# A fused attention and two-expert-layer kernel: another written-out order for its first block, three value sums made on TensorE, two second products in split form, routing's vector work pinned in place

## The chip, the cores and the metric

The program runs on one core of a Trainium2 chip. The metric is the device time of one execution in microseconds (us). Before the change the median of 3 runs is 1375.94 us (1375.69 to 1376.54). Engines are named as the profile names them: PE (TensorE matmuls), PEld (its weight loads), DVE (VectorE), ACT (ScalarE), POOL (GpSimd) and SP (SyncE, which issues all the DMAs here).

## The reference, cut to what matters

Attention over pooled keys and values, a dense layer pair with softplus, then a layer of 8 experts of which each token takes the best one:

```python
# q, k, v: 8 batches x 8 heads x 576 x 64; k_p and v_p: means over 8 neighbours, so 72 keys
scores = scale * q @ k_p.T;  attn = softmax(scores);  a = attn @ v_p
x = a as 4608 tokens x 512
h = x @ w_in                                   # 512 x 2048
g = maximum(h, 0) + log1p(exp(-abs(h)))        # softplus
x = g @ w_out                                  # 2048 x 512
logits = (x / |x|) @ (emb / |emb|).T / tau     # 8 experts
idx = argmax(logits);  gate = max softmax(logits)
out = gate * (maximum(x @ w1[idx], 0) @ w2[idx])   # 512 x 1024 x 512
```

## The kernel before, in words

The 4608 tokens go in 9 blocks of 512. A product of two float32 matrices is made of parts rounded to the fp32r type: a value is its high part plus a rest, and `three` (lines 655 to 658) makes three fp32r matmuls, low by high, high by low and high by high. A matmul on whole float32 operands shows in the trace as two PE records.

For each block `mm1` makes h chunk by chunk (16 chunks of 128 of the 2048 columns; 12 matmuls of 512 columns a chunk), `softplus` (lines 669 to 694) runs over ACT (abs, exp, ln) and DVE, and `mm2` adds g times w_out into four PSUM tiles `acc`. Two PSUM buffers hold h, so the third chunk in a row waits for the softplus of the first. In block 0 every chunk is "full" (`FULL`, line 1169): softplus ends after one DVE addition (L686), and `mm2` multiplies the unrounded float32 g and w_out (L710, four matmuls a chunk). In later blocks g is split (DVE L689, ACT L691, DVE L693) and w_out too (`split_wo`: ACT L634, then DVE or POOL L638), and `mm2` takes `three`.

The first block also prepares everything: it loads q, k and v, sums k and v over 8 neighbours (`add`: on DVE as one reduction, L186, or on POOL as a tree of three additions, L200 to L202, chosen by the table `ALT`), makes masked sums and rounds them (`prep_v` and `build_v` make VH and VL; `prep_r` and `build_r` make RV from the 16 keys of each pair of heads that do not fit in 128 rows), transposes q and k on PE, makes scores and softmax (`score`), and multiplies by the values (`av`, into `pv`, whose result ACT and DVE split into the first input x, L436 and L438). It also turns the 64-bit weights of both dense layers into float32 (`conv_in`, `conv_out`: long chains on DVE, ACT and POOL, lines 587 to 628). All this is cut into small steps; the string `ORDER` lists them in the order in which the instructions are put on all engines, so each engine runs them in that order. A letter is a kind (K keys, B transposed keys, V and W values, R and U left-over values, Q, S scores, E, T, X attention output, I and O weights, M first product, G softplus, Z w_out's split, P second product, lower case a load, H a transpose of the identity that keeps PE working while it would wait). The last two second products of block 0 are not in the string; the main loop makes them among block 1's first products.

From block 1 on, PE and SP follow the code's order; a scheduler orders DVE, ACT and POOL. `route` (lines 758 to 799) turns a block's logits into gates and expert choice by some 15 tiny DVE instructions with one POOL instruction (L768, a square root by power) among them; after the last dense block it runs while the expert layer's first products (`mm3s`, PSUM tiles m, DVE lines 1042 to 1060) are under way.

The few lines that carry the argument:

```python
    def mm2(blk, fc):                     # block 0: float32 operands; else three fp32r products
        ...
            if full:
                nc.tensor.matmul(accs[blk][d], wof[fc][:, dd], f32(g)[:, 0, :], ...)
            else:
                three(accs[blk][d], w[:, 0, dd], w[:, 1, dd], g[:, 0, :], g[:, 1, :], ...)
```

Of the kernel before, what the change touches and what calls it, by code (L numbers as in the profile page):

```python
# [20 lines left out]
def tile_attention_moe_moe(  # L21
# [13 lines left out]
    nc = tc.nc  # L35
# [633 lines left out]
    def softplus(blk, fc):  # L669
# [9 lines left out]
        g_t[blk, fc] = g  # L679
        if alt(f"G{fc}.relu") and blk == 0:  # L680
# [78 lines left out]
    def route(blk):  # L759
# [408 lines left out]

    FULL = tuple(range(NFC))
# [12 lines left out]
    ORDER = """  # L1182
        k0.0 k0.1 l0 q1 K0 q0 H H H H H H H H H H H H H H H H H H H H H H H H H H H H H H H H Q1 K0 r0 k1.0 K0
        K0 K0 K0 K0 H H B0 Q1 q2 B0 Q0 B0 k1.1 B0 R0 S1 q3 S1 R0 S1 Q0 S0 K1 S0 S1 S1 v0.0 S1 Q2 K1 S1 Q2 S0
        K1 S0 H H H H H H S2 H H Q3 S2 l1 S1 U0 S0 S1 U0 Q3 S2 i6 H S3 S0 S2 U0 S1 K1 S1 S2 S3 S0 E1 S3 S2 S0
        K1 E1 q4 v0.1 K1 S2 K1 S0 H H H T1 V0 T1 S3 S0 S3 I6 T1 S2 S3 H H H B1 Q4 B1 I6 B1 S2 Q4 T1 V0 i0 B1
        I6 S3 S0 i2 V0 q5 V0 H H H H H H H H H S4 T1 q6 E0 E0 S2 S4 i3 I0 o6 T0 H H H H H H H H H H Q5 S3 S4
        T1 S3 T0 S4 q7 S4 I0 I0 i8 T0 S4 S2 W0 T0 Q6 o0 W0 U0 W0 T0 S4 r1 S3 W0 T0 i9 S4 I6 H H H H X1 i13 Q5
        S4 E2 X0 S3 Q6 I6 E3 X2 I2 I8 E2 X1 E3 X0 X2 I0 X1 X3 X0 X3 S4 X2 T2 T2 T2 X3 T3 T3 T2 Q7 v1.0 S6 T2
        T3 I0 T2 S4 i11 S6 T3 T3 T3 S6 I6 S5 X4 E4 I0 E4 Q7 I0 X4 S6 X5 S6 X6 i12 X5 X4 S6 I2 I9 o2 X5 X7 I2  # L1190
        X6 M0 X7 X6 T4 I6 X7 I8 I2 M0 R1 T4 T4 I11 O0 R1 T4 I2 S6 I12 M6 S6 T4 I2 T4 I13 S7 I13 O6 o13 S6 T4
        S5 I13 i10 S5 G6 G6 I13 I2 S5 U1 S5 O6 S6 M0 X10 G6 M0 S6 T4 I13 X10 G0 G0 X10 X9 X11 G6 T4 X11 S7 O6
        S7 S5 I13 G0 O0 - X11 E6 I8 X9 T4 S5 E6 v1.1 O13 V1 I11 O2 M2 O0 i7 G0 T6 o1 O2 I13 X9 O13 I3 O2 S7 O6
        M13 O13 O6 O0 S7 I11 I8 P6 O0 I10 I9 G2 V1 G13 P6 G2 I10 O2 I8 I7 I8 O2 I10 I9 o9 G2 o8 G13 I9 I12 I9
        G2 i5 I9 G13 P0 I9 S7 i4 S5 I11 P0 I10 O8 O9 P2 O8 P2 O9 O1 S5 O13 M9 X8 O8 I7 I4 I8 O13 I12 I4 G13 S7
        U1 I3 I10 o7 P13 M8 X8 O9 O8 O9 S5 I10 X8 O8 I5 T6 I10 G9 V1 O9 G9 S5 G9 o10 G9 P13 o11 G8 T6 I11 T6
        G8 U1 I11 E5 O7 S7 G8 I7 O11 I12 M10 O10 E5 P9 U1 G8 P9 O1 O7 G10 I11 T6 O10 O11 I7 O11 O10 I4 I5 G10
        I5 O10 G10 I7 I7 I12 T6 P8 V1 W1 I7 O10 M11 W1 G10 o4 S7 G11 T5 I4 S7 O1 T5 W1 G11 o5 I12 M7 G11 O1 I4
        O4 W1 G7 I12 P8 O7 O11 O7 I4 I4 i1 T5 G11 O4 S7 P10 O7 I3 M4 T5 G7 T5 G7 O11 T5 X14 o12 O5 O4 X14 O1
        O12 i14 O4 P11 O12 G4 G7 I14 X14 I14 O12 X13 I3 I5 I1 O4 E7 I1 X13 X15 I5 I14 I5 G4 O5 O5 G4 O5 G4 M12  # L1200
        P7 I3 X13 o3 P10 X12 O12 I1 X15 O3 X12 G12 G12 P11 P4 O3 E7 O5 X15 T7 O12 X12 I1 T7 i15 I1 I5 O3 I14
        T7 T7 T7 O3 M5 P4 I3 I14 G12 G5 G12 T7 X18 O3 I14 X16 X18 I15 o15 X16 G5 O15 I3 G5 I15 I15 M3 X16 q8
        G5 X19 P5 I15 I1 G3 I1 M1 I15 P5 O15 I14 X18 G3 G3 I15 X19 G3 I15 G1 o14 X17 M15 O14 X19 O14 G1 G1 G1
        G15 O14 M14 O15 P7 P3 P3 P12 P12 P1 O15 X17 O15 X17 G15 P1 G15 G14 G15 G14 G14 O14 O14 G14
    """
    ALT = """
        B0.c1 B1.c1 B1.c2 E0.e0 E0.e1 E1.e0 E1.e1 E2.e0 E2.e1 E3.e0 E3.e1 E5.e0 E5.e1 E6.e0 E6.e1 E7.e0 I1.mul
        I1.sub I10.mul I10.sub I11.mul I11.sub I12.mul I12.sub I13.mul I13.sub I14.mul I14.sub I15.mul I15.sub
        I2.mul I3.mul I3.sub I4.mul I4.sub I5.mul I5.sub I7.mul I7.sub I8.mul I8.sub I9.mul I9.sub K0.m0 K0.m1
        K0.s0 K0.s2 K1.m1 K1.s0 K1.s1 K1.s2 O0.mul O1.mul O10.mul O11.mul O12.mul O13.mul O14.mul O15.mul  # L1210
        O2.mul O3.mul O4.mul O5.mul O6.mul O7.mul O8.mul O9.mul R0.l0 R1.l0 R1.l1 S5.nrm S7.nrm U0.m0 U0.m1
        U1.m0 U1.m1 V0.s0 V0.s1 V0.s2 V0.s3 V1.s0 V1.s1
    """.split()
# [179 lines left out]
```

## Time and profile before

| what | value |
|---|---|
| median of 3 runs | 1375.94 us |
| the profiled execution's own time | 1376.53 us |
| its span, first to last instruction | 1374.7 us |
| mean granted TensorE clock | 0.996 |
| PE busy | 1350.0 us (98%) |
| DVE, ACT, POOL busy | 763.5, 644.5, 281.4 us |
| idle of PE just before an instruction, 8 to 66 us | 6.5 us in 9 waits |

The span is cut by the profile into stretches; a busy PE counts matmuls whose ends are modelled, and the transposes of the identity count as busy as well. Block 0 ends on PE at about 160 us; blocks 1 to 8 and the expert layer fill the rest.

### The profile page before, as it was taken

Reading aid. Unit: us, or ns where it says so; the run is one execution under the profiler, and the core shown is the slowest. Engines: PE = TensorE matmul, PEld = TensorE weight load, DVE = VectorE, ACT = ScalarE, POOL = GpSimd, SP = SyncE. Lnnn points to the kernel's source line nnn. Section 1 sums busy time; section 2 is a strip of 40 time slices with the busy share of each in tenths; the row PEclk is TensorE's granted clock in tenths of the full one; section 3 lists DMA queues with packets and bytes.
Section 4 is the critical chain, followed back from the end, with each engine's and each line's share of the span. In section 5 each row is a group of like instructions: output and inputs, shape, how many; then the busy total and the mean of one; then the engine's idle time right before and its main releaser. Section 6 shows DMA issues by size and latency. Waiting matters only on the chain.

```text
span 1374.7 us, 18505 instructions
## 1 busy us (share of the span) xinstructions
PE 1350.0 (98%) x6998; PEld 1118.0 (81%) x6998; DVE 763.5 (56%) x1608; ACT 644.5 (47%) x1287; POOL 281.4 (20%) x268
## 2 busy tenths in 40 slices
PE   8999999999999999999999999999999999999998
PEld 7666678878888878888888888878878898998986
DVE  7997567566465466475564443353664544544432
ACT  5766455554465464564464454455532322222221
POOL 6500112121021020020020010073353022231100
PEclk9999999999999999999999999999999999999999
DMA  9742354353364363453442242563332212222000
GB/s 275 244 125 85 105 172 140 112 195 107 113 203 124 95 195 92 127 181 95 139 153 85 79 152 77 168 210 126 107 124 93 87 37 77 78 93 93 31 31 32
DMA packets 113564, 166.94 MB, mean 121 GB/s; under 512 B 42808, under 2 KB 69432, under 8 KB 113472
## 3 DMA queue, kind: packets, MB, share of 16 engines
q1 hardware_dynamic: 113472, 165.72, 38.2%
q8 instruction: 57, 0.93, 0.3%
q14 instruction: 35, 0.29, 0.1%
HBM read 128.99 MB, written 36.70 MB: 121 GB/s over the span
## 4 chain that ended last, share of the span: by engine, by line
PE 83%; DVE 8%; DMA 3%; POOL 2%; ACT 2%; issue 1%; SPq 1%; POOLq 0%; DVEq 0%; ACTq 0%
PE h L656 8%; PE h L658 8%; PE h L657 8%; PE acc L656 8%; PE acc L658 8%; PE acc L657 8%; PE y L656 5%; PE y L657 5%; PE y L658 5%; PE m L656 4%; PE m L658 4%; PE m L657 4%; PE pp L338 2%; PE acc L710 2%; PE lg L742 1%; DMA wos<-wo 1%
## 5 line engine op out<-in xcount | busy, mean ns | idle before, releaser
L656 PE MATMUL h<-x,wi 128*128 128x512 f32 x576 | 234.9, 408 | 1.2 <-DVE t L689 1.1
L658 PE MATMUL h<-x,wi 128*128 128x512 f32 x576 | 225.7, 392 | 0.0
L657 PE MATMUL h<-x,wi 128*128 128x512 f32 x576 | 225.0, 391 | 0.0
L672 ACT ACTIVATE t<-h 128x512 f32<-128x512 f32 x144 | 86.1, 598 | 229.5 <-PE h L658 222.7
L656 PE MATMUL acc<-g,ring 128*128 128x512 f32 x448 | 177.9, 397 | 0.1
L658 PE MATMUL acc<-g,ring 128*128 128x512 f32 x448 | 174.8, 390 | 0.0
L657 PE MATMUL acc<-g,ring 128*128 128x512 f32 x448 | 174.4, 389 | 0.0
L689 DVE SCALAR_TENSOR_TENSOR t<-h,t 128x512 f32<-128x512 f32 x128 | 87.9, 687 | 147.3 <-ACT t L676 146.1
L656 PEld LDWEIGHTS h<-x,wi 128*128 128x128 f32 x576 | 108.7, 189 | 24.4 <-DVE t L689 1.8
L658 PEld LDWEIGHTS h<-x,wi 128*128 128x128 f32 x576 | 108.4, 188 | 24.2
L657 PEld LDWEIGHTS h<-x,wi 128*128 128x128 f32 x576 | 108.8, 189 | 21.1 <-issue 1.0
L691 ACT CAST g<-t 128x512 fp32r<-128x512 f32 x128 | 79.6, 622 | 86.7 <-DVE t L689 86.6
L693 DVE TENSOR_TENSOR g<-t,g 128x512 fp32r<-128x512 f32 x128 | 92.0, 719 | 50.7 <-ACT g L691 50.6
L656 PE MATMUL y<-w,g 128*128 128x512 f32 x288 | 113.0, 392 | 0.0
L657 PE MATMUL y<-w,g 128*128 128x512 f32 x288 | 112.9, 392 | 0.0
L658 PE MATMUL y<-w,g 128*128 128x512 f32 x288 | 112.9, 392 | 0.0
L658 PEld LDWEIGHTS acc<-g,ring 128*128 128x128 f32 x448 | 84.1, 188 | 18.4
L656 PEld LDWEIGHTS acc<-g,ring 128*128 128x128 f32 x448 | 84.2, 188 | 16.2 <-issue 0.6
L657 PEld LDWEIGHTS acc<-g,ring 128*128 128x128 f32 x448 | 84.2, 188 | 15.8
L358 POOL TENSOR_TENSOR e<-e,sm 128x576 f32<-128x576 f32 x34 | 39.4, 1159 | 270.9 <-DVE sm L355 223.5
L676 ACT ACTIVATE t<-t 128x512 f32<-128x512 f32 x144 | 91.4, 635 | 2.9
L674 ACT ACTIVATE t<-t 128x512 f32<-128x512 f32 x144 | 91.5, 636 | 2.1
(228 smaller groups left out, 2713.9 us busy)
## 6 DMA issues: line engine op xcount, KB each, us to landing
ring<-wos SPq DMA_DIRECT2D x112, 512.0 KB, 3.7
x2s<-x SPq DMA_DIRECT2D x9, 2048.0 KB, 8.3
b<-x2s SPq DMA_DIRECT2D x27, 512.0 KB, 5.2
out_dram<-o SPq DMA_DIRECT2D x36, 256.0 KB, 2.1
st<-in_k_dram SPq DMA_DIRECT2D x16, 512.0 KB, 5.1
q<-in_q_dram SPq DMA_DIRECT2D x32, 256.0 KB, 4.3
st<-in_v_dram SPq DMA_DIRECT2D x16, 512.0 KB, 6.7
st<-in_moe_w_in_dram SPq DMA_DIRECT2D x16, 512.0 KB, 7.0
```

What stands on the lines that cost most here:

```text
L338: nc.tensor.matmul(pp[p0:p0 + n, i, :], qT[:, j, p0:p0 + n], kbd_t[b][:, j, :], start=True, stop=True)
L358: eng.tensor_tensor(e, e, sm1.unsqueeze(2).to_broadcast([P, H, SP]), ALU.mult)
L656: nc.tensor.matmul(ps, ll, rh, start=first, stop=False, skip_group_check=more)
L657: nc.tensor.matmul(ps, lh, rl, start=False, stop=False, skip_group_check=more)
L658: nc.tensor.matmul(ps, lh, rh, start=False, stop=last, skip_group_check=more)
L672: nc.scalar.activation(t, h, AF.Abs)
L674: nc.scalar.activation(t, t, AF.Exp, scale=-1.0)
L676: nc.scalar.activation(t, t, AF.Ln, bias=1.0)
L689: nc.vector.scalar_tensor_tensor(t, h, 0.0, t, ALU.max, ALU.add)
L691: nc.scalar.copy(g[:, 0, :], t)
L693: nc.vector.tensor_tensor(g[:, 1, :], t, f32(g)[:, 0, :], ALU.subtract)
L710: nc.tensor.matmul(accs[blk][d], wof[fc][:, dd], f32(g)[:, 0, :], start=first, stop=(fc == NFC - 1))
```

## The change

The written-out order and the table of choices are new throughout. Beside them four things change in the code. `values` and `left_values` can make the sums over 8 neighbours on PE, as eight accumulating float32 matmuls by the identity into PSUM (`pe_sum`), from which ACT and DVE make VH, VL and RV directly; the table asks for it for batch 0's values (two sums, `V0.pe`) and left-over values (one, `R0.pe`). `is_full` is now false for chunks 14 and 15 (`P14.z P15.z`), so these two second products of block 0 take split operands. In `route` the first DVE instruction of each part is kept in program order. Of the table of choices, three subtractions of `conv_in` fewer stand on DVE, and batch 1's values and left-over values move from POOL to DVE in part, batch 1's keys to POOL.

```diff
@@ first block
+    def pe_sum(dst, src):
+        n = src.partition_size()
+        for e in range(POOL):
+            nc.tensor.matmul(dst, ident[0:n, 0:n], src[..., e * D:(e + 1) * D], start=(e == 0), stop=(e == POOL - 1))
...
+    def values(b):
+        if not alt(f"V{b}.pe"):
+            yield from prep_v(b)
+            yield from build_v(b)
+            return
+        vs = ps_tile([P, NJ, D], "vsum")
+        for i in range(2):
+            pe_sum(vs[:, 2 * i:2 * i + 2, :], st_t["v", b, i])
+            yield
+            yield
+        for hh in range(2):
+            nc.scalar.activation(VH[:, :, hh, :], vs, AF.Copy, scale=hm[:, hh:hh + 1])
+            yield
+        for hh in range(2):
+            nc.vector.scalar_tensor_tensor(
+                VL[:, :, hh, :], vs, hm[:, hh:hh + 1], f32(VH)[:, :, hh, :], ALU.mult, ALU.subtract
+            )
+            yield
...
@@ mm2 and softplus
     def is_full(blk, fc):
-        return blk == 0 and fc in FULL
+        return blk == 0 and not alt(f"P{fc}.z")
...
@@ route
-        nc.vector.tensor_scalar(n, n, 1e-6, taut, ALU.add, ALU.mult)
+        pin(nc.vector.tensor_scalar(n, n, 1e-6, taut, ALU.add, ALU.mult))
...
-        nc.vector.tensor_reduce(m, z, AX.X, ALU.max)
+        pin(nc.vector.tensor_reduce(m, z, AX.X, ALU.max))
...
-        nc.vector.tensor_scalar(eq, z, 0.0, None, ALU.is_ge)
+        pin(nc.vector.tensor_scalar(eq, z, 0.0, None, ALU.is_ge))
...
-        nc.vector.tensor_reduce(m, rev, AX.X, ALU.min)
+        pin(nc.vector.tensor_reduce(m, rev, AX.X, ALU.min))
...
-        nc.vector.tensor_reduce(n, z, AX.X, ALU.add)
+        pin(nc.vector.tensor_reduce(n, z, AX.X, ALU.add))
...
@@ ORDER, its first line
-        k0.0 k0.1 l0 q1 K0 q0 H H H H H H H H H H H H H H H H H H H H H H H H H H H H H H H H Q1 K0 r0 k1.0 K0
...
+        Z4 Z0 k0.0 K0 Z2 k0.1 K0 l0 K0 q0 K0 K0 q1 q2 H H H H H H H H H H H H H H H H H H H H H H H H H H H H
...
@@ ALT, its last line
-        U1.m0 U1.m1 V0.s0 V0.s1 V0.s2 V0.s3 V1.s0 V1.s1
+        S7.nrm V0.m0 V0.m1 V0.pe V0.s0 V0.s1 V1.s0 Z0.d Z1.d Z10.d Z11.d Z12.d Z2.d Z3.d Z5.d
```

What this does to the order of instructions is shown at three places. The lines named in the pieces of the changed kernel are its own: its L448, L454, L374, L285 and L391 are L395, L401, L321, L268 and L338 of before, its L1095 to L1113 are L1042 to L1060, its L1079 is L1026, its L823 is L770, and L742, L746, L779, L188 and L691 are L689, L693, L726, L186 and L638.

On PE, before, ahead of the first attention output (pm and pl are transposed probabilities, pq a transposed q, idle the transposes of the identity, pv the attention output):

```order
L395 MATMUL pm<-ident,e_262 128x128 x4
L1221 MATMUL idle<-ident 128x128 x10
L321 MATMUL pq<-ident,q_425 128x128 x4
L401 MATMUL pl<-ident,el_449 96x128 x2
L321 MATMUL pq<-ident,q_447 128x128 x4
L1221 MATMUL idle<-ident 128x128 x4
L422 MATMUL pv<-aH,VL 128x256
```

And the stretch that stands ahead of it on PE in the changed kernel (vsum are the sums on PE, pk the transposed keys of batch 1, pp scores):

```order
L454 MATMUL pl<-ident,el_369 96x128 x2
L1275 MATMUL idle<-ident 128x128 x4
L254 MATMUL vsum<-st,ident 128x128 x8
L285 MATMUL pk<-ident,km_423 128x128 x4
L288 MATMUL pk_441<-ident,klm 128x64
L254 MATMUL vsum<-st,ident 128x128 x8
L391 MATMUL pp<-kbd_218,qT_457 64x144
```

The idle transposes there have made room for the sums of batch 0's values, and batch 1's keys are transposed between the two; the scores of the tile that holds both batches stand behind the second sum.

On DVE, before, at the last block's routing (c and g belong to the expert layer's products; n, z, m without a number are routing's):

```order
L1042 TENSOR_TENSOR c_8915<-m,c_8906 128x256
L1026 SCALAR_TENSOR_TENSOR g_8930<-m,g_8930 128x256
L1051 TENSOR_TENSOR c_8940<-m,c_8906 128x256
L770 TENSOR_SCALAR n<-n,taut 128x4
L1052 TENSOR_TENSOR c_8940<-m,c_8940 128x256
L771 RECIPROCAL n<-n 128x4
L775 TENSOR_TENSOR z<-z,n 128x32
L778 TENSOR_REDUCE m<-z 128x4
L1057 TENSOR_TENSOR c_8906<-m,c_8906 128x256
```

And where that instruction (now L823) stands in the changed kernel:

```order
L1079 SCALAR_TENSOR_TENSOR g_9196<-c_9205,g_9196 128x256
L1110 TENSOR_TENSOR c_9153<-m,c_9153 128x256
L1113 TENSOR_TENSOR c_9180<-m,c_9180 128x256
L1040 TENSOR_TENSOR T_9280<-bf_8899,T_9280 128x512 x4
L823 TENSOR_SCALAR n<-n,taut 128x4
L1079 SCALAR_TENSOR_TENSOR g_9196<-c_9153,g_9196 128x256
L1079 SCALAR_TENSOR_TENSOR g_9195<-c_9180,g_9195 128x256
L824 RECIPROCAL n<-n 128x4
```

It has moved behind the next step's four T splits, some forty DVE instructions later, and no longer stands between the additions c of the product during which the POOL instruction that it waits for runs.

On DVE, before, at the end of block 0 (x is the block's result, mx and e scores of a later tile, ks key sums of batch 2, t and g softplus of block 1):

```order
L726 TENSOR_TENSOR x_565<-acc_868,x_565 128x512
L344 TENSOR_REDUCE mx<-pp 128x4
L693 TENSOR_TENSOR g<-t,g 128x512
L344 TENSOR_REDUCE mx<-pp 128x4
L346 TENSOR_TENSOR e_1560<-pp,mx 128x288
L726 TENSOR_TENSOR x_565<-acc_869,x_565 128x512
L346 TENSOR_TENSOR e_1560<-pp,mx 128x288
L351 TENSOR_REDUCE sm_1573<-e_1560 128x8
```

And the same place in the changed kernel:

```order
L779 TENSOR_TENSOR x_518<-acc_889,x_518 128x512
L691 TENSOR_TENSOR wo_1611<-wof_119,wo_1611 128x512
L188 TENSOR_REDUCE ks_1614<-st 128x64 x3
L399 TENSOR_TENSOR e_1569<-pp,mx 128x288
L188 TENSOR_REDUCE ks_1614<-st 128x64
L746 TENSOR_TENSOR g<-t,g 128x512
L404 TENSOR_REDUCE sm_1582<-e_1569 128x8
```

The four key sums of batch 2, which stood ahead of the block's result, now stand behind it and ahead of the softplus rest (L746) of block 1's second chunk.

## Rows read from the trace of the kernel before

**Rows 1.** Busy time per stretch: us, then PE, PEld, DVE, ACT, POOL, PEclk, DMA share, GB/s.
```profile
0.00:39.10 39.10, 32.30 (x231) 28.81 (x231) 30.83 (x78) 24.53 (x57) 27.81 (x51) 0.96 1.02 272
39.10:57.40 18.30, 17.02 (x84) 13.97 (x83) 17.45 (x37) 13.59 (x32) 10.53 (x15) 0.91 0.89 309
57.40:113.90 56.50, 55.80 (x192) 33.29 (x190) 55.34 (x105) 37.38 (x72) 2.90 (x1) 1.00 0.40 123
113.90:160.10 46.20, 46.20 (x165) 28.91 (x166) 23.51 (x43) 21.77 (x44) 2.38 (x3) 1.00 0.20 58
49.20:53.10 3.90, 3.87 (x12) 3.12 (x13) 3.82 (x9) 3.90 (x12) 3.23 (x6) 0.56 0.98 347
```

**Rows 2.** PE in order of time: start, us, instruction, count, idle before it.
```profile
10.18 2.14 PE L338 MATMUL pp<-kbd,qT 128*128 128x144 f32 x16
25.85 1.26 PE L1221 MATMUL idle<-ident 128*128 128x128 f32 x10
30.89 0.39 PE L422 MATMUL pv<-aH,VL 128*128 128x256 f32 x1 [1.07 <-DVE VL L302]
39.09 0.40 PE L656 MATMUL h<-x,wi 128*128 128x512 f32 x1
46.87 0.27 PE L422 MATMUL pv<-aH,VL 128*128 128x64 f32 x1 [1.12 <-ACT t L676]
51.33 0.63 PE L656 MATMUL h<-x,wi 128*128 128x512 f32 x1
52.61 0.62 PE L656 MATMUL h<-x,wi 128*128 128x512 f32 x1
134.70 12.18 PE L710 MATMUL acc<-g,wof 128*128 128x512 f32 x28
160.09 1.14 PE L338 MATMUL pp<-kbd,qT 128*128 128x144 f32 x8
166.53 0.39 PE L656 MATMUL acc<-g,wo 128*128 128x512 f32 x1
171.97 0.60 PE L321 MATMUL pq<-ident,q 128*128 128x128 f32 x4
```

**Rows 3.** DVE, 0 to 160 us, by line and shape: count, busy us, mean ns, idle before.
```profile
L609 DVE TENSOR_TENSOR wi<-st,wi 128x512 fp32r<-128x512 f32 x13 | 8.9, 685 | 0.1
L186 DVE TENSOR_REDUCE ks<-st 128x64 f32<-128x512 f32 x7 | 7.0, 1029 | 5.5 <-DMA st<-in_k_dram 5.5
L438 DVE TENSOR_TENSOR x<-pv,x 128x256 fp32r<-128x256 f32 x8 | 3.0, 407 | 0.0
L186 DVE TENSOR_REDUCE klm<-st 64x64 f32<-64x512 f32 x2 | 2.1, 1029 | 0.0
L302 DVE TENSOR_TENSOR VL<-vm,VH 128x512 fp32r<-128x512 f32 x2 | 1.3, 664 | 0.0
L186 DVE TENSOR_REDUCE vl<-st 96x64 f32<-96x512 f32 x1 | 1.0, 1047 | 1.5 <-DMA st<-in_v_dram 1.5
L314 DVE TENSOR_TENSOR RV<-vlm,RV 32x256 fp32r<-32x256 f32 x2 | 0.8, 417 | 0.1
```

**Rows 4.** POOL, 0 to 160 us, by line and shape, the tree's two longer additions.
```profile
L200 POOL TENSOR_TENSOR st<-st 128x256 f32<-128x256 f32 x11 | 8.5, 775 | 2.5 <-DMA st<-in_k_dram 2.5
L201 POOL TENSOR_TENSOR st<-st 128x128 f32<-128x128 f32 x11 | 5.5, 500 | 0.9
```

**Rows 5.** Waits of PE and DVE in order of time, where routing's DVE work stands.
```profile
206.03 0.33 PE L422 MATMUL pv<-aH,VL 128*128 128x128 f32 x1 [1.24 <-DVE x L438]
833.29 0.23 DVE L770 TENSOR_SCALAR n<-n,taut 128x4 f32<-128x4 f32 x1 [0.31 <-POOL n L768]
1019.47 1.24 DVE L770 TENSOR_SCALAR n<-n,taut 128x4 f32<-128x4 f32 x1 [0.22 <-POOL n L768]
1021.09 0.39 PE L656 MATMUL m<-b,a 128*128 128x256 f32 x1 [0.81 <-DVE c L1052]
1025.91 0.38 PE L656 MATMUL m<-T,a 128*128 128x256 f32 x1 [1.64 <-DVE c L1042]
```

More of the change, by code (lines that the diff above doesn't have):

```diff
@@ L181, in load_q, with pool_sum @@
         q_t[t] = qt
-    def pool_sum(dst, src, pin):
+    pin = tc.keep_in_program_order
+    def pool_sum(dst, src, pinned):
         ins = nc.vector.tensor_reduce(dst, src.rearrange("p (e d) -> p d e", e=POOL), AX.X, ALU.add)
-        if pin:
-            tc.keep_in_program_order(ins)
+        if pinned:
+            pin(ins)
     def rows(a, b):
@@ L245, in fetch_vl @@
             nc.sync.dma_start(st[32 * i:32 * (i + 1)], src)
-        for g in range(2):
-            st_t["vl", b, g] = st[:, g, :]
-    def prep_k(b):
-        ks = kp.tile([P, NJ, D], F32, tag="ks", name=f"ks{b}")
-        for j in range(NJ):
-            add(ks[:, j, :], st_t["k", b, j // 2][:, j % 2, :], f"K{b}.s{j}")
-            yield
-        add(klm[:, 1, :], st_t["kl", b][0:64, :], f"K{b}.s4")
-        yield
+        st_t["vl", b] = st
+    def pe_sum(dst, src):
+        n = src.partition_size()
+        for e in range(POOL):
+            nc.tensor.matmul(dst, ident[0:n, 0:n], src[..., e * D:(e + 1) * D], start=(e == 0), stop=(e == POOL - 1))
+    def prep_k(b):
+        if alt(f"K{b}.pe"):
+            ks = ps_tile([P, NJ, D], "ksum")
+            for i in range(2):
+                pe_sum(ks[:, 2 * i:2 * i + 2, :], st_t["k", b, i])
+                yield
+                yield
+            kl = ps_tile([64, D], "klsum")
+            pe_sum(kl, st_t["kl", b][0:64, :])
+            (nc.scalar.copy if alt(f"K{b}.s4") else nc.vector.tensor_copy)(klm[:, 1, :], kl)
+            yield
+        else:
+            ks = kp.tile([P, NJ, D], F32, tag="ks", name=f"ks{b}")
+            for j in range(NJ):
+                add(ks[:, j, :], st_t["k", b, j // 2][:, j % 2, :], f"K{b}.s{j}")
+                yield
+            add(klm[:, 1, :], st_t["kl", b][0:64, :], f"K{b}.s4")
+            yield
         km = tp.tile([P, NJ, 2, D], F32, tag="wf", bufs=2, name=f"km{b}")
@@ L290, in prep_r @@
         for g in range(2):
-            add(vl[:, g, :], st_t["vl", b, g][0:96, :], f"R{b}.l{g}")
+            add(vl[:, g, :], st_t["vl", b][0:96, g, :], f"R{b}.l{g}")
             yield
@@ L309, in build_r @@
             part = vlm.rearrange("p (j g) d -> p g j d", g=2)[:, :, jj, :]
-            times(part, vl, lm[0:96, jj:jj + 1], b, "A" if alt(f"U{b}.m{jj}") else "G")
+            times(part, vl, lm[0:96, jj:jj + 1], b, "A" if alt(f"R{b}.m{jj}") else "G")
             yield
@@ L315, in build_r, with left_values @@
         yield
+    def values(b):
[4 more added lines that the diff above has]
+        vs = ps_tile([P, NJ, D], "vsum")
+        for i in range(2):
+            pe_sum(vs[:, 2 * i:2 * i + 2, :], st_t["v", b, i])
+            yield
+            yield
+        for hh in range(2):
+            nc.scalar.activation(VH[:, :, hh, :], vs, AF.Copy, scale=hm[:, hh:hh + 1])
+            yield
+        for hh in range(2):
+            nc.vector.scalar_tensor_tensor(
+                VL[:, :, hh, :], vs, hm[:, hh:hh + 1], f32(VH)[:, :, hh, :], ALU.mult, ALU.subtract
+            )
+            yield
+    def left_values(b):
+        if not alt(f"R{b}.pe"):
+            yield from prep_r(b)
+            yield from build_r(b)
+            return
+        vl = ps_tile([96, 2, D], "vlsum")
+        pe_sum(vl, st_t["vl", b][0:96])
+        yield
+        yield
+        for jj in range(2):
+            nc.scalar.activation(RV[0:96, 2 * jj:2 * jj + 2, 1, :], vl, AF.Copy, scale=lm[0:96, jj:jj + 1])
+            yield
+        for jj in range(2):
+            part = RV[64:96, 2 * jj:2 * jj + 2, 1, :]
+            nc.vector.scalar_tensor_tensor(part, vl[64:96], lm[64:96, jj:jj + 1], f32(part), ALU.mult, ALU.subtract)
+            yield
     def qtrans(t):
@@ L679, in softplus @@
         g_t[blk, fc] = g
-        if alt(f"G{fc}.relu") and blk == 0:
+        if alt(f"G{fc}.relu") and is_full(blk, fc):
             nc.scalar.activation(f32(g)[:, 0, :], h, AF.Relu)
@@ L1162, in rest @@
             nc.sync.dma_start(rows_t, o[:, 0, :])
-    FULL = tuple(range(NFC))
     OTHERS = {mybir.EngineType.DVE, mybir.EngineType.Pool, mybir.EngineType.Activation}
@@ L1176, in tile_attention_moe_moe @@
     KINDS = {
-        "K": prep_k, "B": kT, "V": prep_v, "R": prep_r, "W": build_v, "U": build_r, "Q": qtrans, "S": score,
+        "K": prep_k, "B": kT, "V": values, "R": left_values, "Q": qtrans, "S": score,
         "E": spread, "T": atrans, "X": lambda n: av(n // 4, n % 4), "I": conv_in, "O": conv_out, "M": lambda fc: mm1(0, fc),
@@ L1188, in tile_attention_moe_moe @@
[L1188 to L1192, printed above, removed]
@@ L1205, in tile_attention_moe_moe @@
+        O11 G13 q8 G12 G12 Z14 G11 G13 G10 P11 P11 Z8 G0 G11 Z11 G11 G8
     """
     ALT = """
[L1207 to L1210, printed above, removed]
@@ L1230, in first_block @@
                 warm()
-            elif o[0] == "Z" and int(o[1:]) in FULL:
+            elif o[0] == "Z" and is_full(0, int(o[1:])):
                 continue
```

46 lines of the change are left out of this document (28 added, 18 removed).

## The prediction, written before the changed kernel was run

> **What bounds the kernel now.** I read the stretches first, then PE in order of time, then DVE and POOL by shape, then the waits in the rest of the program. The reader should see in the stretches [rows 1] that block 0 has three parts. Up to 39.1 us PE is shown busy for 32.3 us, but this counts the warming transposes; DVE has 30.8 us there. From 57.4 to 113.9 us PE and DVE are both full (55.8 and 55.3 us of 56.5). From 113.9 to 160.1 us PE alone is full and DVE has half its time free. So in block 0 the end is set by PE's work after its first product, which starts at 39.09 us [rows 2], and by when that product can start; DVE decides the latter, and for 56 us runs level with PE. Block 0's last matmul gives way at 160.09 us to scores of a later tile [rows 2]: 121.0 us from the first product. After that PE has hardly a gap. The exceptions that a change of routing can touch are 1.24 us at 206 us and 0.81 + 1.64 us at 1021 and 1026 us [rows 5].
>
> **Part 1, up to the first product.** PE's order has the same things ahead of the product plus three sums. Each is 8 float32 matmuls of 128 columns, 24 in all. The trace has no such matmul; the nearest is a score matmul of 144 columns, 16 records or 8 matmuls in 2.14 us [rows 2], 0.27 us each, so 24 x 0.27 x 128/144 = 5.7 us. The 21 warming transposes that go cost 0.126 us each, 10 in 1.26 us [rows 2]: 2.6 us. The net is 3.1 us more on PE, and it fits: of the 32.3 us shown busy [rows 1] all 72 transposes are some 9 us, so PE has over 15 us of the 39.1 to spare. I cost it at nothing; without this cover it is 3.1 us.
>
> What DVE must do before the product shrinks. Counting its instructions in the two orders up to the last subtraction (L438) that the product needs, 83 become 80: three reductions go (one of k to POOL, the left-over keys to POOL, the left-over values to PE: 1.03 + 1.03 + 1.05 us), VL and RV lose their old subtraction (0.66 + 0.42), and two subtractions from PSUM for each come in their place. Those are not in the trace; the subtraction of x from PSUM over 256 elements takes 0.41 us, the smaller ones at most as much, so 1.2 to 1.6 us, of which I take 1.3 [rows 3]. The other changes are one instruction up or down of six kinds and nearly cancel. The sum is -3.1 - 1.1 + 1.3 = -2.9 us. POOL loses five sums of batch 0's values (four of 0.78 + 0.50 us and a short third addition each, and one of the left-over ones) and gains two of the keys [rows 4], so it gets lighter by over 4 us. This matters, since V's last step stood behind these sums: the first attention output waited 1.07 us for VL at 30.89 us [rows 2]. The bytes loaded ahead of batch 0's values are the same in both orders (5504 KB to the second half's end), so the data don't come earlier. What is late next is DVE itself, 2.9 us earlier. I take -2.8 us, the rest lost to instruction overlap. The bounds are -4.6 (POOL's and V's gain in full) and +3.1 (PE's sums in the way).
>
> **Part 2, from the first product to the end of block 0.** Two second products become split. A full one takes 8 of the 28 records in 12.18 us, 3.48 us; two split ones ran from 166.53 to 171.97 us, 2.72 us each [rows 2]. That is -1.5 us, all on PE while PE is full. What they add (two casts and two subtractions each for g and w_out) falls where DVE has half its time free [rows 1]; without that cover it would be 4 x 0.69 us on DVE.
>
> The 121.0 us hold more than work. I see 1.12 us of waiting at 46.87 us, and behind it matmuls at half clock: in 49.2 to 53.1 us the granted clock was 0.56 [rows 1], and three 512-column matmuls took 1.28 us (51.33 to 52.61), while at the full clock 24 such took 5.44 us (166.53 to 171.97), 0.68 per three [rows 2]. Over nine such matmuls that is 1.8 us. Together 2.9 us that need not recur. Will DVE still hold PE? Between the product's last input and the eighth softplus addition DVE's order has 93 instructions instead of 102, over the same 52 us of PE work: four weight subtractions (L609, 0.69 us each) and some five other passes of like size less, VL and RV of the next batch later, two reductions more [rows 3], together about 4 us less. So DVE leads where it ran level, and I give back half of the 2.9 us. Part 2 is -1.5 - 1.5 = -3.0 us, with bounds -5.5 and 0.
>
> Of those four subtractions some went to POOL. In this trace a tiny DVE instruction of routing took 0.23 us at 833 us and 1.24 us at 1019 us, where POOL was in the middle of long additions [rows 5]; so DVE work can be stretched by POOL's. The Trainium skill (Perfetto Trace Analysis, Optimizing Scalar/DVE Operations) says that the two share an SBUF port and that moving work between them might not help. By that rule the lead of 4 us would lose the moved 2.7 us; the trace agrees in part, since POOL gets lighter by more sums than it is given subtractions, and the sum above would lose some 1 us.
>
> **Part 3, the step into block 1.** On DVE four key sums (1.03 us each [rows 3]) now stand ahead of the second chunk's softplus rest. PE has scores and two first products there before it needs it, from 160.09 to 166.53 us, and one second product of 2.72 us [rows 2]: 9.2 us, against four sums, four subtractions of x and some smaller ones on DVE, about 9 us from the moment the first accumulator is done. I take 0; if the cover falls short by all four sums it is +4.1.
>
> **Part 4, routing.** In the last block the instruction L770 waited on DVE for POOL (1.24 us with its stretch), with an addition c queued behind it that PE needed: PE waited 0.81 and then 1.64 us [rows 5]. It now stands some forty instructions later, when POOL is done with it, and the additions come first. Behind it stand then only routing's own steps; their user, the list of remaining work, comes a hundred us later. I take -2.0 of the 2.45 us. For block 0's routing most of the parts move some hundred instructions later as well, out of the DVE burst that made PE wait 1.24 us at 206 us; I take half of it, -0.6. Bounds: -3.7 and 0.
>
> **Sum.** -2.8 - 3.0 + 0 - 2.6 = -8.4 us. The profiled execution took 1376.53 us (its span and 1.8 us around it), so 1368.1; the median of the runs is 0.6 us lower, so 1367.5 us.
>
> **Rivals.**
> - More is gained: V's shorter path counts in full (-4.6), DVE never holds PE (-5.5), both routing waits go (-3.7): 1362.1 us. For it speaks that POOL and ACT get lighter too; against it, that DVE was busy for 17.45 of 18.3 us behind the first product [rows 1] and nothing was free there.
> - PE's sums come into the way: PE takes its instructions in order, and the sums of batch 0's values wait for their data with the scores of a later tile queued behind. Then the first product comes no earlier and the net 3.1 us are on the path, and parts 2 and 4 remain: 3.1 - 3.0 - 2.6 = -2.5, 1373.4 us. For it speaks the order, which puts those scores behind the second sum; against it, that little but warming stood there before, so PE has the time.
> - The pins do not do what they say: the same wait arises in the next step, where POOL works on as well. Then part 4 is about -0.4 and the time 1369.7 us.
> - Slower: the clock. The new order has 21 warming transposes fewer while PE waits for loads. After one wait of 1.12 us the clock stood at 0.56 for 3.9 us [rows 1, 2]. If a like wait precedes the run of six first products that now stands ahead of the first second product, and the low level lasts through their 72 matmuls, each costs 0.2 us more (1.28 against 0.68 us per three): +14.4, so 1381.9 us. It decides for slower than before from 56 such matmuls on. Against it: at 53 us the clock came back after 9. The Trainium skill (TensorE: Matmul & The Clock Gate, Part 1) says that the default state is throttled and activity releases it, and the trace agrees, 0.56 behind a wait and 1.00 in full work.
>
> **How the numbers follow.** The measurement tells 0.2%, 2.75 us, from no change. Chances: the forecast 0.55, with its own range of 1363.5 to 1371.5 (part 1 by 2, part 2 by 2, part 4 by 1 either way); more gained 0.12; sums in the way 0.15; pins without effect 0.10; slower 0.08. Faster is below 1373.2: the forecast, the larger gain, nearly all of the pins' case and a third of the sums' case, 0.82. Same is 0.10, slower 0.08. The range is 1361.5 to 1375.5: it leaves out the slower case and the outer half of the largest gain.
>
> **What would show it.** Right: the first product at about 36 us, scores of the later tile (after the last second product of block 0) at about 154 us, no PE wait over 0.3 us within 10 us of the last logits, less of a wait in the thirty us after block 0's result. Wrong: PE waiting for the sums' data or a granted clock under 0.9 between 20 and 60 us; a wait of PE for L693's counterpart at the start of block 1; PE's waits near 1021 us moved to the next step rather than gone.

## The result and the profile after

The changed kernel took 1364.63 us, the median of 4 runs (1364.43 to 1364.96), against 1376.10 us of the kernel before beside it: a ratio of 0.9914 (95% interval 0.9898 to 0.9930). The profiled execution has a span of 1363.2 us where it was 1374.7. The forecast was 1367.5 us, so the direction and most of the size came out, and 3 us more were gained than forecast.

The stretches of the changed kernel, cut at the same events as [rows 1] (first product, first second product, where DVE stops being full, end of block 0); us, then PE, PEld, DVE, ACT, POOL, PEclk, DMA share, GB/s:

```profile
0.00:36.90 36.90, 33.27 (x253) 30.73 (x254) 28.49 (x75) 22.17 (x52) 21.76 (x41) 1.00 0.97 257
36.90:57.60 20.70, 20.70 (x110) 17.52 (x109) 20.15 (x49) 19.79 (x42) 10.18 (x9) 1.00 0.88 312
57.60:108.00 50.40, 50.40 (x169) 30.01 (x168) 48.88 (x92) 30.64 (x60) 0.00 (x0) 1.00 0.45 140
108.00:151.50 43.50, 43.50 (x175) 29.63 (x174) 23.61 (x47) 22.50 (x47) 2.07 (x2) 1.00 0.24 69
```

Between first product and end of block 0 PE is busy in every microsecond at a granted clock of 1.00, and POOL has nothing at all from 57.6 to 108 us. PE in order of time answers [rows 2 and 5]: the sums, the first attention output (now without a wait), the first product, the end of block 0 and the wait behind it, the first second product of block 1, and the one wait left near the last routing:

```profile
15.85 1.96 PE L254 MATMUL vlsum<-st,ident 96*96 96x128 f32 x16 [0.83 <-DMA st<-in_v_dram]
22.56 1.96 PE L254 MATMUL vsum<-st,ident 128*128 128x128 f32 x16
29.34 0.35 PE L475 MATMUL pv<-aH,VL 128*128 128x256 f32 x1
36.92 0.40 PE L709 MATMUL h<-x,wi 128*128 128x512 f32 x1
151.48 1.14 PE L391 MATMUL pp<-kbd,qT 128*128 128x144 f32 x8
157.93 0.39 PE L709 MATMUL acc<-g,wo 128*128 128x512 f32 x1
196.83 0.33 PE L475 MATMUL pv<-aH,VL 128*128 128x128 f32 x1 [0.60 <-DVE x L491]
1014.56 0.38 PE L709 MATMUL m<-T,a 128*128 128x256 f32 x1 [0.62 <-DVE c L1095]
```

Where the time came from, as differences of such starts: up to the first product 39.09 - 36.92 = 2.2 us; from there to the end of block 0 121.00 - 114.56 = 6.4 us; from the end of block 0 to the last logits 0.6 us (their rows start at 1003.12 and 993.95 us); behind the last logits, to the end of the span, 2.3 us. Together 11.5 us.

### The profile page after: what moved, and what is told of

It reads as the page before. It is cut to its first block, busy times and chain, and to the rows that moved or that the text cites. A ratio compares the mean times of both kernels' runs of the same rounds, so it can differ in the third digit from the quotient of the medians.

```text
span 1363.2 us, 18579 instructions
## 1 busy us (share of the span) xinstructions
PE 1346.5 (99%) x7033; PEld 1121.0 (82%) x7033; DVE 765.7 (56%) x1614; ACT 644.3 (47%) x1286; POOL 274.9 (20%) x253
## 3 DMA queue, kind: packets, MB, share of 16 engines
q1 hardware_dynamic: 113472, 165.72, 38.5%
## 4 chain that ended last, share of the span: by engine, by line
PE 92%; DVE 4%; ACT 1%; POOL 1%; DMA 1%; issue 1%; SPq 0%; POOLq 0%; DVEq 0%; ACTq 0%
PE h L709 9%; PE h L711 9%; PE h L710 9%; PE acc L709 8%; PE acc L711 8%; PE acc L710 8%; PE y L709 5%; PE y L711 5%; PE y L710 5%; PE m L709 4%; PE m L711 4%; PE m L710 4%; PE acc L763 4%; PE pp L391 2%; PE lg L795 1%; PE pq L374 1%
## 5 line engine op out<-in xcount | busy, mean ns | idle before, releaser
L742 DVE SCALAR_TENSOR_TENSOR t<-h,t 128x512 f32<-128x512 f32 x130 | 89.3, 687 | 150.6 <-ACT t L729 149.4
L746 DVE TENSOR_TENSOR g<-t,g 128x512 fp32r<-128x512 f32 x130 | 95.0, 730 | 51.1 <-ACT g L744 50.9
L709 PEld LDWEIGHTS acc<-g,ring 128*128 128x128 f32 x448 | 84.2, 188 | 15.8 <-issue 0.2
L411 POOL TENSOR_TENSOR e<-e,sm 128x576 f32<-128x576 f32 x34 | 39.1, 1151 | 270.9 <-DVE sm L408 201.7
```

The lines of the kernel that those rows point to most:

```text
L411: eng.tensor_tensor(e, e, sm1.unsqueeze(2).to_broadcast([P, H, SP]), ALU.mult)
L709: nc.tensor.matmul(ps, ll, rh, start=first, stop=False, skip_group_check=more)
L742: nc.vector.scalar_tensor_tensor(t, h, 0.0, t, ALU.max, ALU.add)
L746: nc.vector.tensor_tensor(g[:, 1, :], t, f32(g)[:, 0, :], ALU.subtract)
```

## Experiments

All times are medians; the kernel before ran beside each set at 1376.4 to 1376.9 us. "Block 0" below is the stretch from the first product to the end of block 0: 121.0 us before, 114.6 after.

**Taking one part out of the changed kernel, or putting one alone into the kernel before.**

```diff
-        pin(nc.vector.tensor_scalar(n, n, 1e-6, taut, ALU.add, ALU.mult))
+        nc.vector.tensor_scalar(n, n, 1e-6, taut, ALU.add, ALU.mult)
... (so for all five)
```

> The changed kernel with the five routing pins taken out, nothing else. Theory (pins hold routing's DVE work away from POOL's square root, and that is worth 2.7 us: 0.6 behind block 0, 2.1 behind the last block): about 1367.3 us, with PE waits of some 0.8 and 1.6 us near 1010 us as in the kernel before, and the wait behind block 0's result at 1.2 us instead of 0.6. Rival (those waits went because the work before them came 9 us earlier, or because the scheduler of DVE, ACT and POOL found another order, not by the pins): 1364.6 us within 0.5, waits as in the changed kernel.

1368.37 us, ratio to before 0.9931 (0.9918 to 0.9945). PE's rows behind block 0 and at the last routing are those of [rows 5] again:

```profile
199.01 0.33 PE L475 MATMUL pv<-aH,VL 128*128 128x128 f32 x1 [1.24 <-DVE x L491]
1014.40 0.39 PE L709 MATMUL m<-b,a 128*128 128x256 f32 x1 [1.30 <-DVE c L1105]
1019.22 0.38 PE L709 MATMUL m<-T,a 128*128 128x256 f32 x1 [1.65 <-DVE c L1095]
```

and DVE has its routing instruction back in front of those additions (L1105 follows it), waiting and stretched:

```profile
1012.79 1.23 DVE L823 TENSOR_SCALAR n<-n,taut 128x4 f32<-128x4 f32 x1 [0.72 <-POOL n L821]
```

The theory holds, the rival falls. The time is 3.7 us more than the changed kernel's, but not all of that is the pins: in the profiled execution the first product began at 38.46 us, 1.5 us late, and what the pins can touch, from the end of block 0 on, is 3.0 us longer.

```diff
-        nc.vector.tensor_scalar(n, n, 1e-6, taut, ALU.add, ALU.mult)
+        tc.keep_in_program_order(nc.vector.tensor_scalar(n, n, 1e-6, taut, ALU.add, ALU.mult))
... (so for all five, in the kernel before)
```

> The kernel before with the five routing pins alone. Theory (pins are worth 2.7 us by themselves): 1373.4 us, no wait of PE over 0.7 us near 1021 us, 0.6 us instead of 1.24 at 206 us. Rival (only together with the new order): 1376 us within 0.5, the waits 0.81 and 1.64 us as before.

1372.79 us, 0.9963 (0.9950 to 0.9977). From the last logits to the end of the span it takes 369.2 us, as the changed kernel (369.2; before and without pins 371.6 and 371.8). At the last routing PE waits once:

```profile
1023.48 0.38 PE L656 MATMUL m<-T,a 128*128 128x256 f32 x1 [0.45 <-DVE c L1042]
```

By the traces the pins are worth 2.5 to 3.0 us in either order (by the medians 3.7 and 4.1).

```diff
-        ... P14.z P15.z R0.l1 R0.pe R1.m0 ... V0.m1 V0.pe V0.s0 ...
+        ... P14.z P15.z R0.l1 R1.m0 ... V0.m1 V0.s0 ...
```

> The changed kernel with batch 0's value sums and left-over value sums back on POOL and DVE, in the same written-out order. Theory (the sums on PE are what shortens the path to the first product): first product at 39 us or later instead of 36.9, granted clock or waits at its start worse, 1366.5 to 1369 us. Rival (the new order alone moved the first product, and the sums cost PE 5.6 us that it now gets back): first product at 36 us or earlier, 1364 us or less.

1374.31 us, 0.9978 (0.9969 to 0.9987): of 11.5 us 2.6 are left, about what the pins give. PE, at the first attention output, the first product and behind it:

```profile
34.67 0.55 PE L475 MATMUL pv<-aH,VL 128*128 128x256 f32 x1 [4.20 <-DVE VL L319]
44.48 0.40 PE L709 MATMUL h<-x,wi 128*128 128x512 f32 x1
61.10 0.63 PE L448 MATMUL pm<-ident,e 128*128 128x128 f32 x4 [1.40 <-ACT t L727]
```

The new order without the sums is worse than the old one up to the first product (44.5 against 39.1): VL is 4.2 us late. The table of the changed kernel leaves two of batch 0's four value sums on DVE here (all four were on POOL before), and VL stands behind the second of them, which DVE ends at 31.2 us; POOL's own were done at 28.6. Block 0 itself stays shorter than before, 117.5 us against 121.0.

```diff
     def prep_v(b):
+        if b == 0:
+            vs = kv_t[b] = sums()[:, 0:NJ, :]      # a PSUM bank of the h pool, free until then
+            for i in range(2):
+                pe_sum(vs[:, 2 * i:2 * i + 2, :], st_t["v", b, i])
...
```

> The kernel before, in its own written-out order, with the three sums of batch 0's values made on TensorE and VH, VL and RV taken from PSUM, as in the changed kernel; all idle transposes stay. Theory (the sums take the values' chain off POOL and DVE, and that by itself moves the first product and gives DVE its lead): first product at about 37 us instead of 39.1, the wait of 1.1 us at 47 us and the half clock behind it gone or smaller, 1370 to 1374 us. Rival (sums and new order are worth something only together; the old order is paced by DVE's softmax work before the first product): first product at 38.7 us or later, the wait at 47 us still there, 1375.5 us or more.

1378.63 us, 1.0013 (1.0004 to 1.0022), a little slower than before; the rival holds. The sums stand at 18 to 28.5 us in PE's row:

```profile
17.97 1.91 PE L282 MATMUL sums<-st,ident 96*96 96x128 f32 x16
23.00 1.95 PE L282 MATMUL sums<-st,ident 128*128 128x128 f32 x16
26.50 2.05 PE L282 MATMUL sums<-st,ident 128*128 128x128 f32 x16
34.95 0.36 PE L465 MATMUL pv<-aH,VL 128*128 128x256 f32 x1 [1.07 <-DVE VL L323]
43.04 0.39 PE L699 MATMUL h<-x,wi 128*128 128x512 f32 x1
```

In the chain of waits of this kernel up to the first product the sums have 12.8%: the second and third stand in front of a transposition and of scores that softmax needs, the first in front of ACT's work on RV and q. So the first product begins at 39.1 us with neither, 43.0 with the sums alone, 44.5 with the order alone, 36.9 with both.

```diff
-        ... O9.mul P14.z P15.z R0.l1 ...
+        ... O9.mul R0.l1 ...
```

> The changed kernel with chunks 14 and 15 of block 0 back on whole float32 operands. Theory (a split second product takes 2.72 us against 3.43 us of a full one, all on PE): end of block 0 at 152.9 instead of 151.5 us and 1366.0 us. Rival (hidden: something else sets the end of block 0, for example DVE's splitting of the result or the first softplus of block 1): 1364.6 us within 0.4.

1365.15 us, 0.9913 (0.9900 to 0.9927): in the time no difference can be seen. In the trace block 0 is 115.98 us, 1.42 us longer, as expected; but this execution was shorter in other places: 24.8 us from the end of block 0 to its logits where the changed kernel takes 25.2 (both values occur with the old order too: 25.2 in the kernel before, 24.8 with the sums alone, so this is not the split's doing), and 0.8 us behind the last logits. The term holds in its place; at the end the medians differ by 0.5 us, which the spread covers.

**How much lead DVE has in block 0.** Two runs of the changed kernel with DVE work added, four passes and one:

```diff
-            nc.vector.scalar_tensor_tensor(f32(g)[:, 0, :], h, 0.0, t, ALU.max, ALU.add)
+            for again in range(2 if fc in (13, 0, 2, 6) else 1):      # in the second run: fc == 2
+                nc.vector.scalar_tensor_tensor(f32(g)[:, 0, :], h, 0.0, t, ALU.max, ALU.add)
```

> The changed kernel with four more DVE passes: softplus's last addition of chunks 13, 0, 2 and 6 of block 0 is made twice (0.69 us each, 2.75 us in all, between 45 and 65 us). Theory (the new order gives DVE a lead of 2.75 us or more over TensorE in block 0): no wait of TensorE over 0.15 us between 37 and 151 us, end of block 0 at 151.5 us, 1364.6 us. Rival (DVE leads by little, the waits are gone by the last microsecond): waits that sum to 1.5 to 2.75 us between 45 and 110 us, and 1366 to 1368 us, more if the granted clock falls behind one.

> The changed kernel with one more DVE pass of 0.69 us: softplus's last addition of chunk 2 of block 0 is made twice. Theory (the new order leaves DVE no lead at all, it is only just in time): 115.2 us or more from the first product to the end of block 0 instead of 114.6, and 0.7 to 1 us more in all. Rival (a lead between 0.7 and 2.7 us, which four passes used up): no wait of TensorE behind the first product, 114.6 us, 1364.6 us.

Four passes: 1368.33 us, 0.9937 (0.9923 to 0.9950), block 0 118.7 us, so 4.2 us for 2.75 us of DVE work. PE's waits:

```profile
45.22 0.47 PE L709 MATMUL h<-x,wi 128*128 128x512 f32 x1 [0.49 <-DVE g L740]
49.70 0.47 PE L709 MATMUL h<-x,wi 128*128 128x512 f32 x1 [1.11 <-POOL wi L662]
56.77 0.40 PE L454 MATMUL pl<-ident,el 128*96 128x128 f32 x2 [0.21 <-DVE e L399]
58.45 0.47 PE L709 MATMUL h<-x,wi 128*128 128x512 f32 x1 [1.29 <-DVE g L740]
```

One pass: 1365.42 us beside 1364.35 of the unchanged one, block 0 116.0 us, 1.4 more for 0.7 (the two times alone lie within each other's spread; the trace tells them apart), with these waits:

```profile
55.60 0.40 PE L454 MATMUL pl<-ident,el 128*96 128x128 f32 x2 [0.23 <-DVE e L399]
56.57 0.47 PE L709 MATMUL h<-x,wi 128*128 128x512 f32 x1 [0.56 <-DVE g L740]
```

The added passes are not all that DVE got. In both runs they push another pass, L677, beside a subtraction on POOL. In the changed kernel it begins at 51.78 us, ahead of that subtraction (52.41), and takes 0.68 us. In the run with one added pass it begins 0.04 us behind it and ends 0.55 us after it:

```profile
52.84 1.83 DVE L677 SCALAR_TENSOR_TENSOR wof<-wof,st 128x512 int32<-128x512 int32 x1
52.80 1.32 POOL L662 TENSOR_TENSOR wi<-st,wi 128x512 fp32r<-128x512 f32 x1 [0.86 <-ACT wi L659]
```

So DVE was set back by 0.69 + 1.15 = 1.8 us with one pass and by 2.75 + 1.15 = 3.9 us with four, and block 0 became 1.4 and 4.2 us longer: 0.8 to 1.1 us for each microsecond of DVE. The lead at this place is some 0.4 us (1.8 - 1.4). That PE never waits in the changed kernel doesn't mean that DVE is ahead; it is hardly more than just in time.

**Does moving subtractions from DVE to POOL shorten block 0?** The kernel before with three of them moved:

```diff
-        ... I13.mul I13.sub I14.mul ... I4.mul I4.sub I5.mul ... I8.mul I8.sub I9.mul ...
+        ... I13.mul I14.mul ... I4.mul I5.mul ... I8.mul I9.mul ...
```

> The kernel before with three weight subtractions (L609 for chunks 4, 8 and 13 of w_in, 0.69 us each on DVE) moved to POOL, as the changed kernel has them; nothing else. Theory (in block 0 DVE paces TensorE to about 114 us, so the 2.1 us that DVE no longer has are TensorE's): 119 us or less from the first product to the end of block 0, instead of 121.0, smaller waits at 47 and 65 us, 1374 to 1374.5 us. Rival (only the order as a whole gives it; or POOL's slower subtraction, 1.3 us, comes late or stretches DVE's work beside it): 120.5 us or more, 1376 us or more.

1376.36 us, 0.9998 (0.9990 to 1.0007), block 0 120.7 us: nothing that can be told from noise. The waits on g only moved and grew (0.68 at 53.65, 1.38 at 64.90 us, where it was 0.63 in the kernel before). First DVE, then POOL of this kernel at that place:

```profile
58.90 0.68 DVE L602 SCALAR_TENSOR_TENSOR st<-st 128x512 int32<-128x512 int32 x1
60.97 1.58 DVE L599 SCALAR_TENSOR_TENSOR st<-st 128x512 int32<-128x512 int32 x1
62.58 1.67 DVE L602 SCALAR_TENSOR_TENSOR st<-st 128x512 int32<-128x512 int32 x1
```

```profile
59.11 2.89 POOL L638 TENSOR_TENSOR wo<-wof,wo 128x512 fp32r<-128x512 f32 x1 [5.62 <-ACT wo L634]
61.96 1.74 POOL L609 TENSOR_TENSOR wi<-st,wi 128x512 fp32r<-128x512 f32 x1
```

The reader is to see the ends: L599 ends at 62.55, 0.55 us after POOL's first subtraction (62.00); L602 at 64.25, 0.55 us after POOL's second (63.70). These DVE passes take 0.68 us alone; beside POOL they are through only when POOL's instruction is. Over all of block 0 the integer passes took 2.8 us more than their usual 0.68 and 0.42 us in the kernel before and 4.5 us more here, so of the 2.1 us taken off DVE it got 1.7 back as holding.

**The wait at 47 us and the half clock behind it.** In the kernel before, six more matmuls in block 0's first chunk:

```diff
-            three(h, wi[fc][:, 0, c, :], ..., c == 0, c == KC - 1)
+            n = 3 if blk == 0 and fc == 0 and c == KC - 1 else 1
+            for k in range(n):
+                three(h, wi[fc][:, 0, c, :], ..., c == 0, c == KC - 1 and k == n - 1)
```

> The kernel before, with TensorE kept busy through its wait of 1.12 us at 46.9 us: the last three matmuls of block 0's first chunk are issued three times, so six more matmuls (1.4 us) stand where it waited, and that chunk's sum holds its last quarter three times over. Theory (the half clock of 49.2 to 53.1 us comes from that wait, and costs 1.7 us by itself): granted clock 1.00 there, three 512-column matmuls in 0.69 and not 1.28 us, and 1.4 - 1.1 - 1.7 = -1.4 us: 1374.5 us. Rival (the clock falls for another reason, as the 64-column matmuls behind the wait): clock still near 0.56, and the time 1376 us or more.

1375.79 us, 0.9993 (0.9984 to 1.0003). I had misplaced them: the chunk's last step stands behind the attention output that waits, so the wait stayed (1.13 us at 46.39) and the six came after it. But the clock did not fall (row of the stretch, columns as above):

```profile
49.20:53.10 3.90, 3.90 (x23) 3.37 (x23) 3.45 (x10) 3.87 (x11) 2.79 (x5) 1.00 0.82 289
```

and block 0 was 120.35 us, 0.65 shorter with 1.4 us more work. That is no proof that the wide matmuls kept the clock up: the kernel with the three subtractions moved has the old order on PE and a wait of 1.12 us in the same place, and a granted clock of 1.00 in 48.7 to 52.6 us, while the kernel before with pins had 0.59 in 49.2 to 53.1 us. When the clock falls behind such a wait stays open.

**A version that beats both.** Late in block 0 DVE has much free time (busy for 23.6 of the last 43.5 us), so more second products can be split there (chunks 11 and 12; in the second run 5 as well). The order's end was rewritten: the casts and subtractions of g and w_out go ahead of those products, those of w_out 14 and 15 behind them.

```diff
-        ... G5 X19 O12 M15 Z15 P9 ... P5 G1 P5 P12 P12 ... G11 G13 G10 P11 P11 ...
+        ... G5 X19 O12 Z12 G12 Z12 G12 M15 P9 ... P12 P12 P5 P5 G15 G15 O11 G11 Z11 G11 Z11 G11 P11 P11 Z14 Z14 Z15 Z15 ...
-        ... P14.z P15.z ... Z11.d Z12.d ...
+        ... P11.z P12.z P14.z P15.z ...
```

> The changed kernel with two more second products of block 0 in split form (chunks 11 and 12 beside 14 and 15; their casts and subtractions on ACT and DVE put ahead of them, the splits of w_out 14 and 15 behind). Theory (0.71 us less on TensorE each, and DVE is free there): end of block 0 at 150.1 us, and 1.0 to 1.4 us less at the end, 1363.2 to 1363.6 us. Rival (the split g of chunk 11 is late, since its DVE work begins at 132 us and TensorE wants it at 135; or what is won comes back as a wait at the start of block 1): end of block 0 at 150.5 to 151.5 us or a wait of 0.7 us or more behind it, 1364.6 us.

> The changed kernel with five second products of block 0 in split form: 5, 11 and 12 beside 14 and 15. Theory (0.71 us less on TensorE for each; DVE still has room before 130 us): 112.6 us from the first product to the end of block 0 against 113.3 with four, and 1361.8 to 1362.2 us. Rival (there DVE is full, two more passes of 0.7 us on it make TensorE wait; or the buffer that w_out 11 takes comes free too late): 113.3 us or more and a wait between 110 and 140 us, 1362.5 us or more.

> The changed kernel once more, beside the five-product version on the same chip: 1364.6 us within 0.7, so that the version with five lies 2 to 3 us under it if the split counts in full, within 1 us if it doesn't.

Four split products: 1362.51 us, 0.9894 (0.9878 to 0.9909), block 0 113.3 us, 1.3 less than 114.6. Five: 1363.45 us, 0.9900 (0.9886 to 0.9914), block 0 114.4 us, with a new wait. It is the wait that the rival forecast, but the profile does not show the buffer as its cause: ACT's cast of chunk 11's w_out waited for the last step of that chunk's conversion on DVE (L680), and DVE's subtraction (L691) and PE followed:

```profile
135.12 0.68 DVE L680 SCALAR_TENSOR_TENSOR wof<-st,wof 128x512 int32<-128x512 int32 x1
135.89 0.62 ACT L687 CAST wo<-wof 128x512 fp32r<-128x512 f32 x1 [1.41 <-DVE wof L680]
137.38 0.47 PE L709 MATMUL acc<-g,wo 128*128 128x512 f32 x1 [1.37 <-DVE wo L691]
```

The changed kernel again: 1364.35 us, 0.9909 (0.9896 to 0.9922), first product at 37.49 us, block 0 114.58 us. The four-product version is the fastest by its median and by its trace; its interval still meets that of the changed kernel.

## Why the prediction was right or wrong

**Part 1, -2.8 forecast, -2.2 in the profile.** The size came out, and the sums' price too (1.96 to 2.05 us for each sum of 8 matmuls, 6.0 for the three, against 5.7 estimated). The reason was incomplete. I counted three DVE instructions fewer and read POOL as slack; but the sums alone cost 3.9 us and the order alone 5.4. As far as these two runs show, what pays is that the sums take the values off POOL and DVE while the order puts them where no softmax step waits behind them. "PE's sums come into the way" was the right rival for the old order. Its sign, PE waiting for the sums' data, also appears in other executions of the new one. In the repeat of the changed kernel PE waits so, and the first product comes at 37.5 us:

```profile
23.07 2.02 PE L254 MATMUL vsum<-st,ident 128*128 128x128 f32 x16 [1.31 <-DMA st<-in_v_dram]
```

So the 2.2 us are one pair of executions. In the runs with the new order and the sums the first product begins between 36.4 and 38.5 us, in those with the old order and the old sums between 38.6 and 39.1.

**Part 2, -3.0 forecast, -6.4 measured: the step that failed.** It lies outside the bound of -5.5; the total stayed in its range because the other parts came out near their values. The split term was right (1.42 against 1.5). What failed is giving back half of the 2.9 us on the ground that DVE might hold PE again, and the step under it, that DVE would gain by the number of its instructions. Seen from PE, everything went: the wait at 46.9 us and the small ones at 49.2 and 65.1, 2.0 us in all (I had counted 1.1); the half clock, 1.7; and 1.3 us that remain, which no wait row shows and whose cause stays open. I had also read DVE's full stretch up to 113.9 us as one that runs level with PE. Behind the wait at 65.1 us it limits nothing: PE works on there at full clock with hardly a gap, in the kernel before as well (columns as in [rows 1]):

```profile
39.10:65.70 26.60, 24.69 (x102) 17.19 (x101) 25.48 (x50) 19.43 (x43) 13.43 (x16) 0.94 0.75 252
65.70:113.90 48.20, 48.12 (x175) 30.08 (x173) 47.30 (x92) 31.53 (x62) 0.00 (x0) 1.00 0.40 123
```

Seen from DVE, my "lead of 4 us" did not come, though the count of instructions up to the eighth softplus addition was right (102 and 93); the runs with added work found 0.4 us. What changed is how long DVE's passes take: in block 0 DVE is busy for 96.3 us before and 92.6 after, with 183 and 186 instructions, and POOL for 15.8 and 12.3, with 19 and 11. DVE by shape from the first product to 113.9 us, the kernel before:

```profile
L602 DVE SCALAR_TENSOR_TENSOR st<-st 128x512 int32<-128x512 int32 x12 | 9.3, 783 | 0.1
L599 DVE SCALAR_TENSOR_TENSOR st<-st 128x512 int32<-128x512 int32 x12 | 8.9, 759 | 0.1
L597 DVE TENSOR_SCALAR st<-st 128x512 int32<-128x512 int32 x13 | 6.1, 483 | 0.0
```

and the changed one to 109.0 us, the same three lines:

```profile
L655 DVE SCALAR_TENSOR_TENSOR st<-st 128x512 int32<-128x512 int32 x12 | 8.4, 697 | 0.1
L652 DVE SCALAR_TENSOR_TENSOR st<-st 128x512 int32<-128x512 int32 x12 | 8.1, 691 | 0.0
L650 DVE TENSOR_SCALAR st<-st 128x512 int32<-128x512 int32 x12 | 5.3, 445 | 0.0
```

12 x (86 + 68 + 38 ns) = 2.3 us are passes that POOL no longer holds up (and there is one of them fewer). How such a pass comes to stop PE is shown by the wait at 65.1 us of the kernel before. POOL's L638 ends at 63.16 us and DVE's L599 beside it 0.55 us later; two passes behind that stands the addition g for which PE waits:

```profile
60.26 2.90 POOL L638 TENSOR_TENSOR wo<-wof,wo 128x512 fp32r<-128x512 f32 x1 [7.52 <-ACT wo L634]
62.13 1.58 DVE L599 SCALAR_TENSOR_TENSOR st<-st 128x512 int32<-128x512 int32 x1
64.35 0.68 DVE L686 SCALAR_TENSOR_TENSOR g<-h,t 128x512 f32<-128x512 f32 x1
65.09 3.70 PE L710 MATMUL acc<-g,wof 128*128 128x512 f32 x8 [0.63 <-DVE g L686]
```

L599 was held for 0.9 us, PE waited 0.63; the changed kernel has nothing on POOL there and no wait. In the same way L602 takes 1.64 us at 47.40, beside POOL's L358, ahead of the x for which PE waits 0.17 us at 49.23. What the wait at 46.9 us hung on is not settled: the profile names ACT's t here and DVE's e in two other runs of that order.

How much of the 5.0 us (6.4 - 1.4) the held passes are can only be estimated. At 0.8 to 1.1 us on PE for one on DVE, 2.3 us make 1.8 to 2.5. The half clock may be up to 1.7 more, but the run with the three subtractions moved had a clock of 1.00 at that place and its block 0 still took 120.7 us. The rest is open, and no run took the held passes alone out of the kernel before. That moving subtractions to POOL is not enough by itself is shown, for the old order, by the run that did only this.

The prediction did weigh the rule on this, but on one side: it set POOL's lighter load against the cost of the subtractions moved there, and did not count it as a gain for DVE. The Trainium skill (SBUF — State Buffer, SBUF: two separate sides) states it more sharply than the page cited there: of a DVE instruction with two SBUF inputs and a GpSimd one that reads SBUF, the one that starts first locks the shared ports for the whole instruction, and the other blocks. The trace agrees: the held passes of 1.58, 1.67 and 1.83 us shown here all end 0.55 us after POOL's instruction.

**Part 3, 0 forecast.** Right: from the end of block 0 to the first second product 6.44 us before [rows 2] and 6.45 after. The four key sums are covered: from the end of block 0 to its logits it is 25.2 us before and after.

**Part 4, -2.6 forecast, -0.6 - 2.3 measured.** Right in mechanism and size; both pin runs say the same. The waits of 0.81 and 1.64 us became one of 0.62, and 1.24 became 0.60.

**Rivals.** The clock, the slower case, did not appear: 1.00 throughout block 0. That the pins would do nothing falls by both pin runs. "More is gained" had the nearest time (1362.1), but its parts 1 and 4 were too large and its part 2 too small.

## What to carry to other kernels

An engine with no waits may be just in time rather than ahead: add a known piece of work to the engine that feeds it and see what it costs before you count on a lead, and look in the trace whether the added piece made another pass longer too. Before moving work between DVE and POOL, look for DVE passes of twice their usual length and check whether they end with a POOL instruction; where they do, what DVE gives to POOL can come back as holding, as 1.7 of 2.1 us did here. A new unit for a job and a new order can each lose alone and win together, so test both ways before crediting one.

## What the runs showed of the hardware

Unexpected: integer DVE passes of 0.68 us took 1.58 and 1.67 us beside POOL's subtractions, which took 2.89 and 1.74 us themselves, where L609 has a mean of 1.31 us on POOL in the kernel before. Where a pass with two inputs is held, its end is 0.55 us behind POOL's in each of the rows here, and a start 0.04 us behind POOL's instead of ahead of it made 1.83 us out of 0.68. And the same PE order with a like wait, 1.1 to 1.6 us at 47 us, was followed by a granted clock of 0.56 or 0.59 in two executions and of 1.00 in another.
